# Turning q and k by transposing DMAs in place of TensorE transposes, in a windowed attention with a feed-forward layer

## The chip, the cores and the metric

The kernel runs on one core of a Trainium2 chip. A core has a matrix engine (TensorE, PE in the profile, its weight loads PEld), a vector engine (VectorE, DVE), an activation engine (ScalarE, ACT), GpSimd (POOL) and SyncE (SP), each with a queue of its own that is worked off in order, and 16 DMA engines that all queues share. SBUF is the memory that all engines work from, PSUM the one that TensorE writes into. The metric is the device time of one execution in microseconds, the median of several runs.

## The reference, cut to what matters

Eight batches of attention with eight heads, 576 positions and 64 channels per head. The first four heads see the last 32 positions; the other four see every fourth of the last 128. Then a feed-forward layer from 512 to 2048 channels and back, with SiLU in between.

```python
scores = scale * np.matmul(q, k.transpose(0, 1, 3, 2))
rel = pos[:, None] - pos[None, :]
mask_plain = (rel >= 0) & (rel < window)                      # window = 32
mask_dil = (rel >= 0) & (rel < window * dilation) & (rel % dilation == 0)   # dilation = 4
...
attn = attn / (np.sum(attn, axis=-1, keepdims=True) + 1e-09)
return np.matmul(attn, v).astype(np.float32)
...
x = np.ascontiguousarray(attn_out.transpose(0, 2, 1, 3)).reshape(B * S, H * D)
h = x @ w_in
g = h * (1.0 / (1.0 + np.exp(-h)))
return (g @ w_out).astype(np.float32)
```

Inputs and the output are float32; the kernel computes its matrix products in float16 with sums in float32.

## The kernel before, in words

**Layouts.** A score needs q and k with the 64 channels on the partitions. For the plain heads (called `z = 0`) `qT` and `kT` hold two heads one above the other on 128 partitions, and the 576 positions along the free axis. For the dilated heads (`z = 1`) the positions are split into four classes by their remainder modulo 4; `qC` and `kC` hold two classes one above the other on 128 partitions, and the 144 positions of a class along the free axis, so that a dilated head becomes four plain ones. `kT` and `kC` have 32 columns of zeros in front. Each of the four exists twice, and batch `b` uses the one of number `b % 2`. The scores of 32 queries against 64 keys are one small matmul (L324 and L336), 72 for the plain and 80 for the dilated heads of a batch.

**Getting there, before.** `load_qk` (L95) brings q and k of a batch into SBUF with eight DMAs from POOL's queue, which convert to float16. A row of the tile `n` holds 9 (plain) or 12 (dilated) consecutive positions of a head, 2304 or 3072 bytes of the source in one piece. There are two such tiles for q and two for k, so a load waits until the batch before the previous one has been read. `transpose` (L258) turns 64 (or 48) rows at a time on TensorE, into PSUM: 36 transposes for q and 36 for k of the plain heads, 24 and 24 for the dilated ones, all at L274. Four copies for each of `z = 0` and `z = 1`, half on VectorE and half on ScalarE (L278, L287), move the results to `qT`, `kT`, `qC` and `kC` and put the positions in order.

**After the scores.** VectorE scales, masks and takes maxima (L448 to L464), ScalarE takes exponentials, one instruction per 64 columns and one that reads the sum (L496), VectorE divides (L509 to L512). `turn` (L516) transposes the probabilities on TensorE, `values` (L531) multiplies by v, and the result, `xT`, is the input of the feed-forward layer. v comes in with its own DMAs (`load_v`, L123), and parts of it are shifted to other partitions by DMAs from SBUF to SBUF (`shift_v`, L162).

**Order.** The program is written out by hand. For each batch `b` there is a loop of 16 steps of the first feed-forward product (`layer1`, L639, steps 0 to 15) and then of four or five output tiles with four steps each (`layer2`, L694, from step 16). `plan_of(b)` (L737) hangs the attention of the following batches onto these steps: `at(s, fn, ...)` means that `fn` is issued just before step `s`. In the iteration of batch `b` (from 2 on) the second batch after it gets its transposes at steps 14 and 30 and its plain scores at step 17, while the next batch gets its dilated scores at step 10 or 11 and its probabilities, turns and values in between. Iterations 0 and 1 are irregular, since the pipeline fills there. As every engine works its queue in order, a step that has to wait holds what stands behind it on that engine.

**Queues.** All loads are issued from POOL, in program order; also the shifts of v for batches 2 to 7. SP issues the shifts of v for batches 0 and 1 and one DMA per output tile (`store`, L688), which waits for VectorE's copy of that tile (L691); there are five output tiles.

**Batch 0 and batch 1.** Batch 0 has its own way in (`load_qk0`, `transpose0`), and batch 1 uses `load_qk` and `transpose`. The change leaves both as they are.

Of the kernel before, what the change touches and what calls it, by code (L numbers as in the profile page):

```python
# [8 lines left out]
F16 = mybir.dt.float16  # L9
# [6 lines left out]
P = 128  # L16
W = 32
DIL = 4
# [4 lines left out]
HF = P // 2  # L23
UR = DIL
URS = (9, 12)


@with_exitstack
def kernel(
# [9 lines left out]
    nc = tc.nc  # L39
    B, H, S, D = q.shape  # L40
# [3 lines left out]
    HH = H // 2  # L44
# [4 lines left out]
    CL = S // DIL  # L49
    UPS = [S // u for u in URS]  # L50
    HS = S // 2
# [9 lines left out]
    nat = ctx.enter_context(tc.tile_pool(name="nat", bufs=2))  # L61
# [33 lines left out]
    def load_qk(b):  # L95

        for which in (0, 1):
            t = nat.tile([P, H * 8, D], F16, tag=f"n{which}", name=f"n{which}_{b}")
            u0, u1 = 2 * URS[0], 2 * (URS[0] + URS[1])
            qk[b, 0, which] = t[:, 0:u0].rearrange("p (h u) d -> p h u d", h=2)  # L100
            qk[b, 1, which] = t[:, u0:u1].rearrange("p (h u) d -> p h u d", h=2)
        for z in (1, 0) if b == 1 else (0, 1):
            for which, src in ((1, k), (0, q)):
                for i in (0, 1):
                    h = 2 * (2 * z + i)
                    nc.gpsimd.dma_start(  # L106
                        out=qk[b, z, which][i * HF : i * HF + UPS[z]].rearrange("p h u d -> p h (u d)"),
                        in_=src[b, h : h + 2].rearrange("h (p u) d -> p h (u d)", u=URS[z]),
                    )

    def load_qk0(part):

        t0, n = ((0, PA), (SA, PB))[part]
        qk0[part] = [None, None]
        for which, src in ((1, k), (0, q)):
            t = nat.tile([P, H * 8, D], F16, tag=f"n{which}", name=f"n{which}_0{part}")
            t = qk0[part][which] = t[:, 0 : H * UR].rearrange("p (h u) d -> p h u d", h=H)
            nc.gpsimd.dma_start(
                out=t[0:n],
                in_=src[0, :, t0 : t0 + n * UR].rearrange("h (p u) d -> p h (u d)", u=UR),  # L120
            )
# [53 lines left out]
    qk = {}  # L175
# [16 lines left out]
    def clear_v(b, engine):  # L192
# [13 lines left out]
        out=band[0:W], in_=band[0:W], compare_op=ALU.is_ge, fill=NEG,  # L206
# [3 lines left out]
        out=band[0:W], in_=band[0:W], compare_op=ALU.is_ge, fill=NEG,  # L210
# [35 lines left out]
    def att(b):  # L246
        if b not in state:
            state[b] = {
                "qT": qTs[b % 2],
                "kT": kTs[b % 2],  # L250
                "qC": qCs[b % 2],
                "kC": kCs[b % 2],
                "vw": vws[b % 2],
                "xT": xtp.tile([P, HP, S], F16, tag="xT", name=f"xT_{b}"),
            }
        return state[b]

    def transpose(b, z, which, copies):  # L258
# [3 lines left out]
        a = att(b)  # L262
        src, n, ur = qk[b, z, which], UPS[z], URS[z]
        ts = [ps.tile([P, ur, n], F16, tag="ps", name=f"t{which}_{b}_{z}_{i}") for i in (0, 1)]
# [457 lines left out]
    def transposes(at, b, z, step):  # L722
        for which in (1, 0):
            at(step, transpose, b, z, which, both)

    def later(at, b, z, steps, copies=(nc.vector.tensor_copy, nc.vector.tensor_copy)):

        for hi in (0, 1):
            at(steps[hi], normal, b, z, hi)
        for hi in (0, 1):  # L730
            at(steps[2], turn, b, z, hi)
        for hi in (0, 1):
            at(steps[2], turned, b, z, hi, copies[hi])
        at(steps[3], values, b, z)
        at(steps[3], finish, b, z, copies)

    def plan_of(b):  # L737
        ev = {}

        def at(s, fn, *args):  # L740
            ev.setdefault(s, []).append((fn, args))

        def all_exps(b, z):
            for hi in (0, 1):
                at(16, exps, b, z, hi)

        if b == 0:

            at(-16, normal, 0, 1, 1)
            at(-15, shift_class, 0, dve, 1, 2)  # L750
            at(-14, normal, 0, 0, 1)
            at(-13, clear_v, 1, nc.vector)
            at(-13, load_v, 1)
            for c in (2, 3):
                at(-13, load_w_out, c)
            at(-13, load_qk, 2)
            at(-8, turn, 0, 1, 1)
            at(-8, turned, 0, 1, 1, act)
            at(-6, values0, 1, 1)
            at(-6, last_values, 0, 1, (1,))  # L760
            at(-6, finish0, 1, 1)
            at(-6, last_finish, 0, 1, 1)
            at(-4, turn, 0, 0, 1)
            at(-4, turned, 0, 0, 1)
            at(-2, values0, 0, 1)
            at(-2, last_values, 0, 0, (1,))
            at(-2, finish0, 0, 1, both)
            at(-2, last_finish, 0, 0, 1)
            transposes(at, 1, 1, 2)
            at(8, scores, 1, 1)  # L770
            for hi in (0, 1):
                at(8, shift, 1, 1, hi)
            for which in (1, 0):
                at(17, transpose, 1, 0, which, (dve, dve))
            at(20, scores, 1, 0)
            at(14, shift_v, 1, nc.sync.dma_start)
            at(15, load_qk, 3)
            at(15, load_v, 2)
            at(15, shift_v, 2, nc.gpsimd.dma_start)
            all_exps(1, 1)  # L780
            for hi in (0, 1):
                at(20, exps, 1, 0, hi)
            for n, z, hi in ((20, 1, 0), (20, 1, 1), (26, 0, 0), (28, 0, 1)):
                at(n, normal, 1, z, hi)
            for n, z, copies in ((27, 1, (dve, dve)), (30, 0, both)):
                for hi in (0, 1):
                    at(n, turn, 1, z, hi)
                for hi in (0, 1):
                    at(n, turned, 1, z, hi, both[hi])
                at(n + 1 + z, values, 1, z)  # L790
                at(n + 1 + z, finish, 1, z, copies)
        elif b == 1:
            transposes(at, 2, 0, 2)
            transposes(at, 2, 1, 10)
            transposes(at, 3, 0, 15)
            at(7, scores, 2, 0)
            at(17, load_qk, 4)
            at(17, load_v, 3)
            at(17, shift_v, 3, nc.gpsimd.dma_start)
            at(13, scores, 2, 1)  # L800
            all_exps(2, 0)
            all_exps(2, 1)
            at(21, scores, 3, 0)
            at(21, exps, 3, 0, 0)
            at(21, exps, 3, 0, 1)
            later(at, 2, 0, (22, 24, 27, 28))
            later(at, 2, 1, (29, 31, 33, 34))
        else:
            if b + 2 < B:
                at(16, load_v, b + 2)  # L810
                at(16, shift_v, b + 2, nc.gpsimd.dma_start)
            if b + 1 < B:
                if b == 2:
                    for n in (0, 1):
                        at(1 + 2 * n, transpose, 3, 1, 1 - n, both)
                later(at, b + 1, 0, (0, 0, 4, 6))
                if b + 3 < B:
                    at(16, load_qk, b + 3)
            if b + 2 < B:
                transposes(at, b + 2, 0, 14)  # L820
                at(17, scores, b + 2, 0)
                at(18, exps, b + 2, 0, 0)
                at(18, exps, b + 2, 0, 1)
            if b + 1 < B:
                at(10 if b == 2 else 11, scores, b + 1, 1)
                all_exps(b + 1, 1)
                later(at, b + 1, 1, (22, 24, 28, 29) if b == 6 else (22, 24, 27, 28))
            if b + 2 < B:
                transposes(at, b + 2, 1, 30)

        def plan(s):
            for fn, args in ev.pop(s, ()):
                fn(*args)

        return plan
# [58 lines left out]
    for b in range(B):  # L894
        plan = plan_of(b)
        if b == 0:
            for x in range(NFF):
                plan(2 * x - NFF)
                plan(2 * x + 1 - NFF)
                layer1_part(2 * x % NFF, 2 * x // NFF, None if x else warm)  # L900
        else:
            for f in range(NFF):
                plan(f)
                layer1(b, f)
        if b == 0:
            layer2_first(plan)
        else:
            layer2(b, plan)
        for s in range(NFF, 3 * NFF):
            plan(s)  # L910
# [30 lines left out]
```

## Time and profile before

| | |
|---|---|
| median of 3 runs | 325.28 us (325.08 to 325.43) |
| profiled execution, its own time | 324.54 us |
| profiled execution, span of the profile | 322.8 us |
| granted TensorE clock | 0.999 |
| TensorE busy | 311.8 us, 97% |
| ScalarE busy | 214.7 us, 67% |
| VectorE busy | 180.1 us, 56% |
| POOL busy | 83.2 us, 26% |
| transposes at L274 | 840, for batches 1 to 7 |
| DMA packets | 45668, 32.63 MB |

In the profile a line such as `L274 PE MATMUL` names the line of the kernel, the engine and the operation. The slices cut the span into 40 equal parts, a digit gives the busy share in tenths. The chain lists, in order of time, the work that the end waited for: start, duration, engine, tile and line, and how many instructions were merged. A line of the waits gives the total time, the number of waits and the longest one. A line of the table by stretches gives, after the stretch and its length, the busy time and the number of instructions of PE, PEld, DVE, ACT and POOL, then the clock, the DMA share and GB/s.

### The profile page before, as it was taken

To read this page: it belongs to the slowest core of one execution; us is meant where nothing else is said; L and a number is where in the kernel's file an instruction comes from. 1 tells how busy PE (TensorE), PEld (TensorE's weight loads), DVE (VectorE), ACT (ScalarE), POOL (GpSimd) and SP (SyncE) were. 2 spreads that over 40 slices of the span, in tenths; PEclk is the share of its full clock that TensorE was granted. 3 is DMA by queue.
4 is the path that set the end of the run, shared out by engine and by line. 5 is a ranking of instruction groups with operands and counts; after the bars stand their busy time and mean duration, and the time that the engine had idled before them with its cause. 6 is when DMAs were issued, how large, how long until landed. Compare 5 with 4: busy or idle time off the path is not lost.

```text
span 322.8 us, 11769 instructions
## 1 busy us (share of the span) xinstructions
PE 311.8 (97%) x5151; PEld 202.0 (63%) x5151; DVE 180.1 (56%) x379; ACT 214.7 (67%) x700; POOL 83.2 (26%) x140
## 2 busy tenths in 40 slices
PE   5899999999999999999999999999999999999995
PEld 2667754677446775577645776567745776467544
DVE  5896679736597556663665446662576423620011
ACT  1776657657999569965896458975799357736300
POOL 8545537418404430335005700050000000000000
PEclk9999999999999999999999999999999999999999
DMA  8999999938924990298119840191011100110021
GB/s 108 187 212 198 184 230 204 227 99 124 184 86 83 129 146 36 73 163 133 26 68 140 170 80 2 67 174 37 5 52 49 65 4 0 68 67 0 2 97 67
DMA packets 45668, 32.63 MB, mean 101 GB/s; under 512 B 21264, under 2 KB 40336, under 8 KB 45616
## 3 DMA queue, kind: packets, MB, share of 16 engines
q0 software_dynamic: 39520, 21.73, 49.1%
q1 hardware_dynamic: 5952, 10.08, 8.5%
q8 instruction: 40, 0.66, 0.8%
q14 instruction: 12, 0.10, 0.1%
q10 hardware_dynamic: 144, 0.07, 0.1%
HBM read 37.75 MB, written 9.44 MB: 146 GB/s over the span
## 4 chain that ended last, share of the span: by engine, by line
PE 87%; DVE 6%; ACT 3%; issue 1%; POOL 1%; DMA 1%; POOLq 0%
PE h L644 35%; PE o L707 33%; PE h L664 4%; PE t L274 3%; PE x L554 3%; PE pt L521 2%; PE o L681 2%; PE s L336 2%; PE s L324 1%; DVE pn L512 1%; DVE ms L448 1%; ACT pe L496 1%; DVE nm L464 1%; PE x L580 1%; DVE ob L691 1%
## 5 line engine op out<-in xcount | busy, mean ns | idle before, releaser
L707 PE MATMUL o<-w_out,gT 128*128 128x512 f16 (+1 forms) x528 | 115.6, 373 | 0.0
L644 PE MATMUL h<-xT,w_in 128*128 128x288 f16 x896 | 115.4, 286 | 0.0
L652 ACT ACTIVATE gT<-h 128x576 f16<-128x576 f32 x112 | 72.8, 650 | 61.9 <-PE h L644 61.2
L644 PEld LDWEIGHTS <-w_in 128*128 128x128 f16 x896 | 85.7, 98 | 23.0 <-DVE xT L631 0.3
L496 ACT ACTIVATE pe<-ms,nm 128x64 f32<-128x64 f32 x246 | 81.6, 333 | 3.3 <-DVE nm L464 3.2
L707 PEld LDWEIGHTS <-gT 128*128 128x128 f16 x528 | 50.1, 98 | 53.0
L691 DVE COPY ob<-o 128x512 f32<-128x512 f32 (+1 forms) x36 | 24.6, 682 | 52.5 <-PE o L707 52.1
L496 ACT ACTIVATION_READ_ACCUMULATOR pe<-ms,nm 128x1 f32 x246 | 46.0, 187 | 0.0
L448 DVE SCALAR_TENSOR_TENSOR ms<-s,mask 128x512 f32<-128x512 f32 x28 | 19.2, 686 | 41.4 <-PE s L336 25.0
L127 POOL DMA_DIRECT2D vw<-in_v_dram x16 | 10.1, 640 | 76.9 <-PE x L554 75.5
L512 DVE TENSOR_TENSOR pn<-pe,r 128x640 f16<-128x640 f32 (+2 forms) x32 | 25.3, 792 | 1.1
L631 DVE CAST xT<-x 128x512 f16<-128x512 f32 x27 | 17.4, 686 | 12.0 <-PE xs L618 12.0
L464 DVE TENSOR_REDUCE nm<-ms 128x10 f32<-128x640 f32 (+1 forms) x28 | 22.0, 787 | 1.0
L106 POOL DMA_DIRECT2D n<-in_k_dram x28 | 16.5, 602 | 14.6 <-PE t L274 5.2
L106 POOL DMA_DIRECT2D n<-in_q_dram x28 | 16.4, 605 | 10.0 <-DMA w_out<-in_moe_w_out_dram 5.4
L664 PE MATMUL h<-xT,w_in 128*128 128x256 f16 (+1 forms) x128 | 17.9, 295 | 0.5 <-ACT gT L671 0.5
L529 DVE COPY ptT<-pt 128x640 f16<-128x640 f16 (+1 forms) x27 | 11.7, 468 | 8.0 <-PE pt L521 8.0
L664 PEld LDWEIGHTS <-w_in 128*128 128x128 f16 x128 | 12.5, 101 | 4.7 <-issue 1.2
L681 PE MATMUL o<-w_out,gT 128*128 128x512 f16 x64 | 15.1, 380 | 0.0
L671 ACT ACTIVATE gT<-h 128x512 f16<-128x512 f32 (+1 forms) x16 | 10.3, 650 | 7.1 <-PE h L664 6.9
L521 PE MATMUL pt<-ident,pn 128*128 128x128 f16 x152 | 12.4, 224 | 1.4 <-DVE pn L512 1.2
L521 PEld LDWEIGHTS <-pn 128*128 128x128 f16 x152 | 10.1, 99 | 4.7 <-DVE pn L512 1.5
(102 smaller groups left out, 267.6 us busy)
## 6 DMA issues: line engine op xcount, KB each, us to landing
out_dram<-ob SPq DMA_DIRECT2D x35, 256.0 KB, 2.1
n<-in_k_dram POOLq DMA_DIRECT2D x28, 144.0 KB, 5.4
n<-in_q_dram POOLq DMA_DIRECT2D x28, 144.0 KB, 5.5
vw<-in_v_dram POOLq DMA_DIRECT2D x8, 288.0 KB, 6.7
vw<-in_v_dram POOLq DMA_DIRECT2D x16, 128.0 KB, 4.8
w_in<-in_moe_w_in_dram POOLq DMA_DIRECT2D x4, 512.0 KB, 11.6
w_out<-in_moe_w_out_dram POOLq DMA_DIRECT2D x4, 512.0 KB, 10.6
vw<-vw POOLq DMA_DIRECT2D x12, 128.0 KB, 2.8
```

The lines of the kernel that those rows point to most:

```text
L106: nc.gpsimd.dma_start(out=qk[b, z, which][i * HF : i * HF + UPS[z]].rearrange("p h u d -> p h (u d)"), in_=src[b, h : h + 2].rearrange("h ...
L448: nc.vector.scalar_tensor_tensor(out=ms[:, 0:8].rearrange("p (n t) c -> p n (t c)", n=2), in0=s[hi].rearrange("p n t c -> p n (t c)"), sca ...
L464: nc.vector.tensor_reduce(out=nm[:, 0:w], in_=ms[:, 0:w], axis=AX.X, op=ALU.max, negate=True)
L496: nc.scalar.activation(pe[:, t, :], slot(t), AF.Exp, scale=1.0 if b else scale, bias=nm[:, t : t + 1], accum_out=l[:, t : t + 1],)
L512: nc.vector.tensor_tensor(pn[:, 0:w], a["pe", z, hi][:, 0:w], r[:, 0:w, None].broadcast_to([P, w, KB]), ALU.mult)
L521: nc.tensor.transpose(t[:, i, :], a["pn", z, hi][:, 2 * i : 2 * i + 2].rearrange("p t c -> p (t c)"), ident)
L644: nc.tensor.matmul(h[:, half, 0:HS], w_in16[:, c, f * P : f * P + P], xT[:, c, half * HS : half * HS + HS], start=(c == 0), stop=(c == MC ...
L652: nc.scalar.activation(gT[:, f, s0 : s0 + S].rearrange("p (a c) -> p a c", a=2), h[:, :, 0:HS], AF.Silu)
L664: nc.tensor.matmul(h[:, i, 0 : c1 - c0], w_in16[:, c, (f + i) * P : (f + i + 1) * P], xT[:, c, c0:c1], start=(c == 0), stop=(c == MC - 1),)
L681: nc.tensor.matmul(o, gT[:, f, t * P : (t + 1) * P], w_out16[:, f, :], start=(f == 0), stop=(f == NFF - 1),)
L691: copy(ob, o)
L707: nc.tensor.matmul(o, gT[:, f, t * P : (t + 1) * P], w_out16[:, f, m0:m1], start=(f == 0), stop=(f == NFF - 1),)
```

## The change

For batches 2 to 7, `load_qk` and `transpose` are replaced by `load_rows` and `cross`.

`load_rows` keeps the tile `n` and the conversion to float16, but lays it out by rows of tokens. For the plain heads a DMA per head puts position `64 m + p` on partition `p`; the columns are ordered by pair of heads, `m`, head within the pair, channel. Each piece of the source is the 64 channels of one position, 256 bytes. For the dilated heads one DMA puts the positions `4 i` to `4 i + 3` of all four heads on partition `i` for `i` up to 127, and a second one does the last 16, on partitions 64 to 79; the pieces are 1024 bytes. That is six DMAs for k and six for q.

`cross` issues transposing DMAs from SP's queue, from SBUF to SBUF. For the plain heads one DMA for each pair of heads and each of k and q takes 64 rows of 1152 columns, nine groups of 128 columns, and writes the 128 partitions of `qT` or `kT`. For the dilated heads one takes 128 rows of 1024 columns and one the last 16 rows, straight into `qC` or `kC`. That is eight transposing DMAs per batch. TensorE, PSUM, VectorE and ScalarE have no part in it.

In the schedule, `cross` for batch 2 stands at steps 22 and 25 of iteration 0, behind SP's shifts of v for batch 1; for the batch `b + 2` it stands at steps 2 (plain) and 6 (dilated) of iteration `b`. Scores, exponentials and all the rest stay at their steps.

```diff
+RT = 64
...
+    def load_rows(b):
+
+        for which, src in ((1, k), (0, q)):
+            t = nat.tile([P, H * 8, D], F16, tag=f"n{which}", name=f"n{which}_{b}")
+            f = t[0:RT].rearrange("p u d -> p (u d)")[:, 0 : 2 * S // RT * P]
+            f = qk[b, 0, which] = f.rearrange("p (i m h d) -> p i m h d", i=2, h=2, d=D)
+            for h in range(HH):
+                nc.gpsimd.dma_start(
+                    out=f[:, h // 2, :, h % 2], in_=src[b, h].rearrange("(m p) d -> p m d", p=RT)
+                )
+            f = t.rearrange("p u d -> p (u d)")
+            u0, n = 2 * S // RT * P, HH * DIL * D
+            f = qk[b, 1, which] = [f[:, u0 : u0 + n], f[RT : RT + CL - P, 0:n]]
+            for e, (o, i0) in enumerate(zip(f, (0, P))):
+                nc.gpsimd.dma_start(
+                    out=o.rearrange("p (h c) -> p h c", h=HH),
+                    in_=src[b, HH:H].rearrange("h (p r) d -> p h (r d)", r=DIL)[i0 : i0 + o.shape[0]],
+                )
+
+    def cross(b, z):
+
+        a = att(b)
+        for which in (1, 0):
+            f = qk[b, z, which]
+            if z == 0:
+                for i in (0, 1):
+                    o = (a["qT"], a["kT"][:, :, W:])[which][:, i]
+                    nc.sync.dma_start_transpose(
+                        out=o.rearrange("d (m p) -> d m p", p=RT),
+                        in_=f[:, i].rearrange("p m h d -> p (m h d)"),
+                    )
+            else:
+                for i0, g in zip((0, P), f):
+                    o = (a["qC"], a["kC"][..., W:])[which][..., i0 : i0 + g.shape[0]]
+                    nc.sync.dma_start_transpose(out=o.rearrange("d h m i -> d (h m) i"), in_=g)
...
-            at(-13, load_qk, 2)
+            at(-13, load_rows, 2)
...
+            at(22, cross, 2, 0)
+            at(25, cross, 2, 1)
...
-            at(15, load_qk, 3)
+            at(15, load_rows, 3)
...
-            transposes(at, 2, 0, 2)
-            transposes(at, 2, 1, 10)
-            transposes(at, 3, 0, 15)
+            at(2, cross, 3, 0)
+            at(6, cross, 3, 1)
...
-            at(17, load_qk, 4)
+            at(17, load_rows, 4)
...
-                if b == 2:
-                    for n in (0, 1):
-                        at(1 + 2 * n, transpose, 3, 1, 1 - n, both)
...
-                    at(16, load_qk, b + 3)
+                    at(16, load_rows, b + 3)
...
-                transposes(at, b + 2, 0, 14)
+                at(2, cross, b + 2, 0)
+                at(6, cross, b + 2, 1)
...
-            if b + 2 < B:
-                transposes(at, b + 2, 1, 30)
```

## The prediction

> **What bounds the kernel now.** I read the page first, engine shares and slices; then the chain in order of time, for what a transpose costs the engine that sets the end; then the engines' own waits; last the DMA stretches, since the change moves its work there.
>
> ```profile
> PE 311.8 (97%) x5151; PEld 202.0 (63%) x5151; DVE 180.1 (56%) x379; ACT 214.7 (67%) x700; POOL 83.2 (26%) x140
> DMA  8999999938924990298119840191011100110021
> PE 87%; DVE 6%; ACT 3%; issue 1%; POOL 1%; DMA 1%; POOLq 0%
> ```
>
> TensorE works 97% of the 322.8 us span and carries 87% of the chain. The DMA engines are the second thing to watch: nine tenths or more in most slices up to about 65 us, then bursts.
>
> ```profile
> 190.98 3.05 PE h L644 x24
> 194.03 0.76 PE t L274 x72
> 194.78 2.07 PE h L644 x16
> ...
> 209.35 1.83 PE o L707 x8
> 211.18 0.71 PE t L274 x48
> 211.89 1.83 PE o L707 x8
> 213.72 3.92 PE h L644 x32
> ```
>
> This stretch of the chain shows the work that goes: 72 transposes of the plain heads (0.76 us) and 48 of the dilated heads (0.71 us) per batch, squeezed between feed-forward matmuls with no gap. It also shows a restart: 32 uninterrupted matmuls of L644 take 3.92 us (0.1225 each), so 24 should take 2.94 and took 3.05, 16 should take 1.96 and took 2.07. Each switch back costs 0.1 us (the same for L707: 8 take 1.83 against 40 in 8.74).
>
> ```profile
> SPq L692 <- DVE ob L691: 233.1, 29, 23.8
> ...
> POOL vw L127 <- PE x L554: 75.5, 4, 24.4
> ...
> POOL n L106 <- PE t L274: 5.2, 1, 5.2
> ```
>
> The SP queue and POOL mostly wait: SP for output tiles, POOL for buffers of v. Both have room; the only wait of a q or k load on the transposes is one of 5.2 us, at 73 us; it becomes a wait for batch 2's transposing DMAs, with v of batch 3 queued behind it.
>
> ```profile
> 60.00:65.00 5.00, 5.00 (x104) 3.62 (x103) 2.87 (x5) 4.58 (x8) 1.03 (x2) 1.00 1.54 236
> 65.00:70.00 5.00, 5.00 (x109) 3.88 (x108) 0.69 (x1) 3.00 (x5) 1.07 (x2) 1.00 0.51 129
> 70.00:75.00 5.00, 5.00 (x85) 3.93 (x83) 3.73 (x7) 3.67 (x6) 1.90 (x4) 1.00 0.11 10
> ```
>
> The last two columns are the DMA share (packets overlap, so it can pass 1) and GB/s. The initial backlog ends at about 66 us. From there each batch of q, k and v is a burst of some 16 us in 36.
>
> **The change, part by part.**
>
> *Transposes on TensorE removed.* In the chain the groups of batches 2 to 7 are 0.76, 0.70, 0.52 + 0.61, 0.40, 0.40, 0.76, 0.71, 0.76, 0.71, 0.76, 0.71, 0.76 and 0.70 us: 9.26 us for 720 matmuls. They are 13 interruptions, each with a restart of 0.1: 1.3 us more. As TensorE has no idle before them, all 10.6 us is on the path.
>
> *Copies out of PSUM removed.* 48 copies, on VectorE 0.75 us and ScalarE 0.64 us each, four of either per batch: 3.0 and 2.6 us per batch. Worth nothing directly: TensorE hides them. They matter as cover: ScalarE's exponentials fill the second layer (17.64 us busy of the 21 from 157 to 178), and a shorter TensorE could have met them. At the turn after batch 2 ScalarE copies from 137.08 to 138.27, loads its table until 139.56, and then waits 0.60 us for L644. TensorE gives up 0.81 there, ScalarE 1.2: the slack stays. VectorE ends batch 4's probabilities at 142.2, 0.9 us before TensorE turns them at 143.07; both move together, since they follow the same output copy. What is late next is thus the operands of the scores.
>
> *Loads by rows.* Per batch 8 loads become 12. Each plain head is read as 576 pieces of 256 B, 4608 per batch, and the dilated heads as 1152 of 1 KB, instead of 896 pieces of 2.3 or 3 KB. Nearest row: the plain part of v (L140) has 2304 such pieces, takes POOL 1.19 us and landed in 5.1 us where the DMA was quiet (209 to 213 us); L127, 256 pieces of 1 KB, takes 0.63. So on POOL 8 x 0.72 + 2 x 0.70 + 2 x 0.57 = 8.3 us in place of 4.8: hidden, POOL is busy 26%. In transfer, q and k now take about 9 us (145 to 154 us); v's plain pieces took some 4 us, so I take 8.5 + 4 = 12.6 us, 4 more per batch. Bounds: no more (as many bytes) and 2 x 5.1 + 5 = 15 us.
>
> *Transposing DMAs on SP.* Eight per batch: four of 64 x 1152, two of 128 x 1024, two of 16 x 1024. No row shows one. From below they are copies from SBUF to SBUF, as the shifts of v: 0.51 us of the queue and 2.2 us to land. From above each lands before the next begins, at the 5.5 us that such copies took under load: 44 us per batch. By pieces of 256 B there are 4608 a batch; L140's 5.1 us less the 2.2 us floor is 1.26 ns a piece, so 5.8 us of transfer per batch. I take that, with 1.2 us of the queue each (the longest shift, L160 on SP, took 1.22) and a landing of 5.5 us in the backlog, 3 us after it. They are nearest to the shifts: same memory at both ends, same queue.
>
> The Trainium skill (Advanced Engine Details and Errata, X-Bar Transpose (TRN2)) says that transposing DMAs run as fast as plain ones, 350 to 400 GB/s. An estimate from it for 1.18 MB is 3.4 us per batch, and the total would then be about 1.5 us below mine; no run yet shows it.
>
> *SP's queue.* In the steady state the transposes enter right after the last store of the batch before, 8 x 1.2 = 9.6 us, and the next store is due some 20 us into the batch; five output tiles give more room. The plain scores are due at step 17, some 17 us in. Hidden, while four transposes take under about 14 us.
>
> *The beginning is not so roomy.* Due times are those of before less the transposes already gone. Batch 2: loads landed at 54.2 (48.76 + 5.4), now 58; plain operands are there at 57 + 2 x 1.2 + 5.5 = 65, due 67.9; dilated ones at 57 + 8 x 1.2 + 5.5 = 72, due 74.5. Batch 3: loads landed at 60.5, now 4 + 4 for two batches' rows + 6 for batch 2's transposes later, 74.5; operands at 82.4, due 82.6. Batch 3's v hangs behind: POOL shifts v of batch 2 when it lands (66.5, now 80.5), then issues 12 loads of batch 4 to 90, their bytes and the rest of batch 3's transposes last to 98, v of batch 3 to 104, its shifts land at 107.5, and L554 wants them at 106 (109.97 less 3.9). So 1.5 us of stall; bounds 0 (rows at no cost) and 9 (the 14 us of delay come to 22 if loads and transposes cost their upper values). Afterwards POOL waits 12 to 24 us per batch for buffers, and the delay is absorbed.
>
> Sum on the profiled execution: 324.54 - 10.6 + 1.5 = 315.4 us. The median of the runs is 325.28, 0.74 above it: 316.2 us.
>
> **The rivals.**
>
> *Backlog.* The rows and transposes of batches 2 and 3 fill the DMA engines to 100 us or beyond, and TensorE waits 4 to 9 us at batch 3's plain scores or at its values. For: slices at 9 up to 65 us, landings of 6.5 to 13.6 us for q and k loads issued before 46 us. Against: a stall gives its length to every later due time. Worst, 324.54 - 10.6 + 9 + 0.74 = 323.7; typically 321.
>
> *Slower: the transposes pass one after another.* SP issues in order and holds the next until the last has nearly landed. Cost c each: 48 of them from 53 us on, then the 58 us from the dilated scores of the last batch (264.78) to the end: 53 + 48c + 58. It decides from c = 4.45 us, where this is 324.5; at 5.5 it is 375. Below that, c over 3.5 us makes the plain scores late, at step 17. For: in the crowded part the shifts from SP took 5.3 to 7.4 us to land. Against: that is landing time, and the trace shows shifts issued 0.6 us apart. The Trainium skill (VectorE: DVE Perf Modes, The three transpose paths) gives 1309 ns for a 128 x 128 block by DMA against 390 ns on TensorE. If blocks passed one by one, 36 per batch would make 47 us and the whole 53 + 6 x 47 + 58 = 393 us, an estimate that falls on this side; the page does not say whether blocks overlap.
>
> *All hidden.* No stall at all: 314.7 us. For: the lateness above, 1.5 us, is smaller than the error of its terms.
>
> *ScalarE becomes the bound.* It would leave about half the gain, 320 us; the 0.60 us wait and the copies that it loses speak against.
>
> **How the numbers follow.** Forecast (0 to 4 us of stall, all hidden included) 0.54, backlog 0.17, ScalarE 0.02, no change within 0.2% (0.65 us, about what a measurement of this kernel can tell) 0.03, slower through the transposes 0.24. So faster 0.73, same 0.03, slower 0.24. The likeliest alone spans 314.2 to 319. The range goes on through the backlog to a transpose price just past the deciding point: 314.2 to 327; the slow tail beyond it is about 0.19.
>
> **What would show it.** TensorE's groups of L274 shrink to batch 1's 120; its busy time falls by 9 to 11 us; no wait of TensorE on a transposing DMA beyond some 1.5 us at batch 3; a queue time on SP of about 1.2 us per transpose, landing under 6. Wrong if SP holds each transpose for over 3.5 us, if the scores of batches 4 to 7 wait for DMA, if stores queue so long that VectorE waits for output tiles, or if the DMA slices stay at 9 beyond 110 us.

## The result, and the profile after

The changed kernel takes 321.86 us (median of 20 runs, 317.59 to 326.83) against 324.78 us before (20 runs, 323.39 to 326.35). The medians thus differ by 2.9 us. The ratio used here and below leaves out every run that is over 1.5% above the fastest of its kernel; it is 0.9845, with a 95% interval of 0.9816 to 0.9875, so that 5.0 us (4.1 to 6.0) come off. Forecast were 9.1: the change is faster and inside the range, but it gives about half of that, and by the medians a third. The runs of the changed kernel scatter over 9 us, those of before over 3, and part of what follows bears on that. Its profiled execution took 322.74 us, with a span of 321.0.

From the page of the changed kernel: engines (busy time, share, instructions), granted clock and DMA by slices, the DMA queues (packets, MB, share) and the shares of the chain.

```profile
PE 304.5 (95%) x4431; PEld 195.8 (61%) x4431; DVE 163.0 (51%) x355; ACT 201.4 (63%) x676; POOL 106.8 (33%) x164
...
PEclk9999999999999999999879999999999999999999
DMA  8999999999999999799914999279501100110021
...
q0 software_dynamic: 69088, 21.74, 72.7%
q1 hardware_dynamic: 33792, 17.16, 27.1%
q8 instruction: 34, 0.56, 0.7%
...
PE 81%; DVE 6%; DMA 6%; ACT 3%; issue 2%; POOL 1%; SPq 1%; POOLq 0%
```

TensorE has the 720 matmuls less, but its busy time fell by only 7.3 us, and its share of the span from 97 to 95%: it works less and also stands more. Two slices show a lower clock. The DMA engines stay at nine tenths to 160 us, but for one slice, and come back to it from 176 to 200; before, they left that level at 65 us. "issue" has grown to 2% of the chain: time in which the engine waits for nothing that the profile shows.

The stretches that ended the backlog before now do not (same columns, changed kernel):

```profile
60.00:65.00 5.00, 5.00 (x53) 3.51 (x42) 1.69 (x4) 3.93 (x6) 2.45 (x5) 1.00 2.44 141
65.00:70.00 5.00, 5.00 (x109) 3.91 (x107) 1.19 (x2) 2.69 (x5) 2.24 (x4) 1.00 1.88 177
70.00:75.00 5.00, 5.00 (x79) 3.88 (x78) 1.81 (x4) 3.35 (x6) 0.48 (x1) 1.00 1.27 282
```

The share falls from 2.44 to 1.27 only, where it fell from 1.54 to 0.11.

TensorE's waits in the changed kernel (total us, times, longest):

```profile
PE s L361 <- issue: 3.0, 1, 3.0
PE s L373 <- issue: 1.5, 1, 1.5
...
PE s L361 <- DMA qT<-n: 0.6, 1, 0.6
```

The only wait for a transposing DMA is the 0.6 us at the plain scores of batch 3, at 83.2 us. The two long ones have no releaser. The chain of the changed kernel around the longer of them (start, duration, what), and the same pieces of a later batch:

```profile
154.35 0.86 PE o L744 x4
155.21 0.43 PE s L361 x42
155.64 2.99 issue
158.63 0.36 PE s L361 x20
158.99 0.11 PE ss L361 x8
159.09 11.49 PE o L744 x40
...
192.71 5.01 PE h L681 x40
197.72 0.86 PE o L744 x4
198.58 0.61 PE s L361 x64
199.19 0.08 PE ss L361 x6
199.27 8.74 PE o L744 x40
```

In the later batch nothing stands between L744, the 64 scores and L744 again: no transposes, as intended. In the earlier one TensorE stops in the middle of the scores, after 42 of 64, for 2.99 us, and then 40 matmuls of L744 take 11.49 us in place of 8.74. The table by stretches of the changed kernel says why (columns as for the kernel before):

```profile
155.00:156.00 1.00, 0.64 (x43) 0.36 (x42) 0.00 (x0) 0.98 (x2) 0.09 (x1) 1.00 3.21 99
156.00:157.00 1.00, 0.00 (x0) 0.00 (x0) 0.00 (x0) 0.99 (x5) 0.00 (x0) 1.00 8.88 72
157.00:158.00 1.00, 0.00 (x0) 0.00 (x0) 0.00 (x0) 1.00 (x8) 0.00 (x0) 0.91 0.38 21
158.00:159.00 1.00, 0.37 (x30) 0.30 (x30) 0.00 (x0) 1.00 (x8) 0.00 (x0) 0.50 2.41 152
```

The granted clock goes to 0.50, and the trace keeps it there for 6.83 us. In the stall the DMA share is 8.88 at 72 GB/s, and in the next microsecond 21 GB/s are moved: packets that begin there stay open for long. One packet that comes late is TensorE's own. Queue q8 of the page carries packets of 16384 bytes, 34 now and 40 before; TensorE has 8862 matmuls and weight loads now and 10302 before, one packet for each 256. Counting all of TensorE's instructions in the trace from the first (matmuls, weight loads and a few on semaphores), every long "issue" gap of the changed kernel and of its variants below falls on instruction 256 n + 193, at the end of such a block:

```
run                gap, us (length)        instruction       its packet, us   TensorE goes on
changed kernel     112.50-113.96 (1.46)  3777 = 14*256+193   111.39-112.66    1.3 us after it
changed kernel     155.64-158.63 (2.99)  5057 = 19*256+193   155.25-157.10    1.5
b2_wide_loads      204.11-207.62 (3.51)  6081 = 23*256+193   204.54-205.97    1.6
b3_again           112.00-114.17 (2.17)  3777 = 14*256+193   110.83-112.30    1.9
c3_hybrid           63.51- 64.73 (1.22)  2241 =  8*256+193    62.49- 63.47    1.3
d2_plus64           63.70- 67.18 (3.48)  2241 =  8*256+193    64.55- 65.82    1.4
gaps that wait for data: 2809, 2945, 3481 (not of the form 256 n + 193)
```

TensorE had run out of instructions. The packet for the next block leaves some time after the boundary before it: 0.9 us (median) where the DMA engines have room, and up to 160 us in the changed kernel mostly 1.8 to 6.5 us, 3.3 in the median. It then takes 0.9 to 2.3 us, and after a gap TensorE goes on some 1.4 us behind its end. A block that TensorE goes through faster than this round trip ends in a gap. Blocks with scores, turns and values in them are short: the one that ends at 112 us takes some 5 us. The kernel before has blocks as short, 4.8 us up to 63.1 and 3.5 us up to 79.6, but there the packet left 1.8 and 0.7 us after the boundary, and none of its matmuls waits for "issue". What holds a packet back before it leaves, the traces do not show; they show only that it is late where the DMA engines are crowded.

The Trainium skill (Runtime: NRT & Kernel Launch, Instruction fetch mechanics) says that instructions come in blocks of 256 over a DMA queue of the sequencer's own, while the current block runs, at a cost that is mostly hidden. The trace agrees on the size and on the queue; the cost is hidden in the kernel before, and not in the changed one. The Trainium skill (TensorE: Matmul & The Clock Gate, Why this matters for your kernels) warns of idle gaps over some 3 us, behind which the clock is halved. The gap of 2.99 us agrees; of two shorter ones below, 2.13 us in `d1_plus40` was enough as well, for half as long, and 2.17 us in `b3_again` was not.

### The profile page after: what moved, and what is told of

Same layout as the page of the kernel before. It is cut to its first block, busy times and chain, and to the rows that moved or that the text cites. A ratio compares the mean times of both kernels' runs of the same rounds, so it can differ in the third digit from the quotient of the medians.

```text
span 321.0 us, 10444 instructions
## 1 busy us (share of the span) xinstructions
PE 304.5 (95%) x4431; PEld 195.8 (61%) x4431; DVE 163.0 (51%) x355; ACT 201.4 (63%) x676; POOL 106.8 (33%) x164
## 3 DMA queue, kind: packets, MB, share of 16 engines
q1 hardware_dynamic: 33792, 17.16, 27.1%
## 4 chain that ended last, share of the span: by engine, by line
PE 81%; DVE 6%; DMA 6%; ACT 3%; issue 2%; POOL 1%; SPq 1%; POOLq 0%
PE h L681 33%; PE o L744 32%; PE h L701 4%; DMA qT<-n 3%; PE x L591 3%; PE pt L558 2%; DMA n<-in_q_dram 2%; PE o L718 2%; PE s L361 1%; DVE pn L549 1%; PE s L373 1%; DVE ms L485 1%; SPq L139 1%; ACT pe L533 1%; DVE nm L501 1%
## 5 line engine op out<-in xcount | busy, mean ns | idle before, releaser
L744 PE MATMUL o<-w_out,gT 128*128 128x512 f16 (+1 forms) x528 | 117.7, 379 | 0.0
L681 PE MATMUL h<-xT,w_in 128*128 128x288 f16 x896 | 113.8, 286 | 0.0
L744 PEld LDWEIGHTS <-gT 128*128 128x128 f16 x528 | 51.1, 99 | 55.8 <-issue 3.3
L119 POOL DMA_DIRECT2D n<-in_q_dram x24 | 17.8, 774 | 10.4 <-DMA w_out<-in_moe_w_out_dram 5.0
L119 POOL DMA_DIRECT2D n<-in_k_dram x24 | 17.8, 760 | 2.5 <-PE h L701 2.0
```

Source lines behind the costliest of these rows:

```text
L119: nc.gpsimd.dma_start(out=f[:, h // 2, :, h % 2], in_=src[b, h].rearrange("(m p) d -> p m d", p=RT))
L681: nc.tensor.matmul(h[:, half, 0:HS], w_in16[:, c, f * P : f * P + P], xT[:, c, half * HS : half * HS + HS], start=(c == 0), stop=(c == MC ...
L744: nc.tensor.matmul(o, gT[:, f, t * P : (t + 1) * P], w_out16[:, f, m0:m1], start=(f == 0), stop=(f == NFF - 1),)
```

## The experiments

The first three separate the parts of the change: `a0_same` runs it again, `b1_no_cross` takes the transposing DMAs away and keeps the loads by rows, `b2_wide_loads` keeps the transposing DMAs and takes the loads by rows away.

**a0_same.** No edit.

> The changed kernel once more. Theory F (TensorE's own instructions, fetched in 16 KB packets on DMA queue 8, come late where the DMA engines are crowded, and a stall of about 3 us also halves the clock for some 7 us): the spread of 317 to 327 us comes back, with TensorE gaps released by 'issue' at other places than in the first profile (there 1.46 us at 112.5 and 2.99 us at 155.6), each beginning within 1 us of the start of a packet on queue 8. Theory D (the operands come late, always at the same scores): the same gaps at the same places, and times within 1 us of one another.

Measured: 320.6 us (318.58 to 326.15, 6 runs), ratio 0.9848 [0.9822, 0.9875]. TensorE's waits:

```profile
PE s L373 <- issue: 3.5, 1, 3.5
...
PE x L591 <- DMA vw<-vw: 0.9, 1, 0.9
```

One gap without a releaser, 3.47 us at 112.83, again at instruction 3777; its packet started at 113.59, when TensorE already stood. Waits for data are 0.35 us at batch 3's plain scores and 0.88 us at its values. The spread and the late packet are as theory F has them, but the place is one of the first profile's, as theory D has it; only moving the block ends, further below, tells the two apart.

**b1_no_cross.** `cross` issues nothing, so the scores of batches 2 to 7 are computed from what lies in the buffers.

```diff
     def cross(b, z):
-        a = att(b)
-        for which in (1, 0):
+        att(b)
+        for which in ():
```

> Loads by rows as changed, but no transposing DMA at all: the scores of batches 2 to 7 are made from what batches 0 and 1 left in the operands, so the output is not the reference's. What TensorE is spared stays. Theory F with the transposes as the larger part of the crowding: 313.5 to 315 us (324.5 less the 10.6 us), runs within 1.5 us of each other, no gap released by 'issue' over 1 us. Rival R (the small pieces of the row loads alone are the trouble): 316 us and more, gaps by 'issue' remain and the runs spread as before.

Measured: 313.55 us (313.41 to 314.29, 4 runs), ratio 0.9661 [0.9648, 0.9674]. From its page:

```profile
PE 301.0 (97%) x4431; PEld 194.7 (62%) x4431; DVE 163.2 (52%) x355; ACT 201.4 (65%) x676; POOL 106.7 (34%) x164
...
DMA  8999999999995995299319990291011000200021
```

This is the change with no transposes at all: 11.2 us below before, and TensorE's busy time is 10.8 us lower. With the block ends where they are here, rows alone cost TensorE next to nothing. It also gives a yardstick: its matmuls are those of the changed kernel one for one, so each can be held against its twin. What the profiled executions lose against it, by the time at which a matmul falls behind:

```
                           changed kernel       a0_same
waits for data             0.59  (83 us)        0.36 (83) + 1.04 (107)
gap at a block boundary    1.69 (112) + 3.14 (156)   3.70 (112)
half clock behind it       2.81                 2.60
all, to the end            9.2                  8.4
```

Of the 9.2 us, 7.6 are late instructions and the half clock that follows them.

**b2_wide_loads.** The loads of before in pieces of 2.3 and 3 KB, and the same eight transposing DMAs per batch on the bytes that they bring (in an order that is not that of the tokens).

```diff
     def load_rows(b):
+        load_qk(b)
...
+            qk[b, 0, which] = [t[i * RT : i * RT + RT, 0:n] for i in (0, 1)]
+            qk[b, 1, which] = [t[:, 0:g], t[RT : RT + CL - P, 0:g]]
```

> Loads in pieces of 2.3 and 3 KB as in the kernel before, and the eight transposing DMAs of the changed kernel per batch, of the same shapes, from those bytes: the operands are permuted, so the output is not the reference's. Theory F: the crowding is less by the 4 us or more per batch that the rows cost, 314.5 to 317 us, spread about half. Rival X (transposing DMAs themselves, whatever the loads, hold up the instruction fetch): 318 to 322 us with gaps by 'issue' as in the changed kernel. Rival R: 314 to 315 us, no spread.

Measured: 328.7 us (325.52 to 334.27, 7 runs), ratio 1.0074 [1.0049, 1.0099]: slower than before, and above all that was expected. TensorE's waits, and the transposes to `kC`, in the profiled execution, which is the slowest of the seven:

```profile
PE s L352 <- DMA qT<-n: 8.2, 3, 5.3
PE s L352 <- issue: 3.5, 1, 3.5
```

```profile
L136 SPq DMA_TRANSPOSE kC<-n x12: 1222/2116/7707, 58.7 to 235.0; - x12
```

I had taken the rows to be the dearer part. With large pieces SP holds a transpose for up to 7.7 us, and TensorE waits 8.2 us for operands. That small packets of the transposes queue behind large ones of the loads would explain it, but no run separates this.

**b3_copies.** Each transposing DMA is replaced by a plain copy from SBUF to SBUF, in pieces of 256 bytes, from the same queue at the same place; q and k are not turned. The copies carry nine tenths of the bytes, since they leave out one of the nine column groups of the plain heads and a part of the last 16 rows.

```diff
-                    nc.sync.dma_start_transpose(
-                        out=o.rearrange("d (m p) -> d m p", p=RT), ...
+                    nc.sync.dma_start(
+                        out=o.rearrange("p (b c) -> p b c", b=8)[:, :, 0:P], ...
```

> The changed kernel with each of the 48 transposing DMAs replaced by a plain copy from SBUF to SBUF, at the same place of SP's queue, from the same rows to the same operand tiles, in pieces of 256 bytes (8 of the 9 column groups of the plain heads, and of the last 16 rows a part); the operands are thus not turned and the output is not the reference's. Theory T (turning in flight is what makes the DMA engines stand still and TensorE's instruction packets late): 313.5 to 315.5 us, close to the 313.6 us without any such DMA, no gap of TensorE released by 'issue', no stretch in which no DMA packet ends. Rival C (any further traffic of 256-byte packets does it): 318 to 322 us, with gaps by 'issue', as the changed kernel's 320.6.

Measured: 317.41 us (314.66 to 319.05, 4 runs), ratio 0.9757 [0.9716, 0.9798]. It was run again:

> The kernel of b3_copies once more (plain copies in pieces of 256 B in place of the transposing DMAs; what TensorE then computes with is not q and k turned). If plain traffic of this size has a price of its own, 316 to 319 us again, with gaps without a releaser of under 2 us and no stretches in which all packets stand still. If the slower executions of b3_copies were chance, 313.5 to 315, beside b1_no_cross.

Measured: 316.37 us (314.62 to 317.22, 4 runs), ratio 0.9724 [0.9695, 0.9754]. The first of these lines is of `b3_again`'s waits of TensorE, the second of `b3_copies`' copies to `kT` (min, median, max on SP, in ns), the third of the transposes to `kT` in the changed kernel:

```profile
PE s L375 <- issue: 2.2, 1, 2.2
```

```profile
L139 SPq DMA_DIRECT2D kT<-n x12: 596/608/686, 49.4 to 207.9; - x12
```

```profile
L139 SPq DMA_TRANSPOSE kT<-n x12: 1200/1311/4122, 49.3 to 216.5; - x12
```

The 2.2 us are again at instruction 3777; the profile of `b3_copies`, its fastest execution, has 0.4 us there. Both medians lie between what theory T and what rival C had expected. So plain traffic of about this size already makes instructions late and costs 2.8 to 3.9 us against `b1_no_cross`, and turning the bytes another 3.2 to 4.2 against `a0_same`. Two differences can be seen: SP needs twice as long for a plain head's transpose, and there are stretches of over 0.15 us in which at least four packets are open and none ends. The trace has 1 of them before (0.26 us in all), none and 1 with copies, 3 without either (0.48), and 20 (5.3 us) and 16 (4.9) in the two profiles of the changed kernel. That these stretches are what makes the transposes dearer is not shown.

**c1_early.** If the packets are late in the stretch where loads and transposes meet, the transposes of batches 4 to 7 could go earlier.

```diff
+            at(20, cross, 4, 0)
+            at(22, cross, 4, 1)
...
+                    at(20, cross, b + 3, 0)
+                    at(22, cross, b + 3, 1)
...
-                at(2, cross, b + 2, 0)
-                at(6, cross, b + 2, 1)
```

> The changed kernel with the transposing DMAs of batches 4 to 7 issued one iteration earlier, at steps 20 and 22, right behind the row loads of the same batch, so that they no longer run beside the row loads of the next one. Theory F: fewer packets in flight at once, so fewer and shorter 'issue' gaps: 315 to 318 us, most runs at a clock of 1.0. If the crowding is a matter of the sum and not of the overlap: 318 to 322, as the changed kernel. If SP's stores, which now stand behind transposes that wait for their loads, hold VectorE: over 322.

Measured: 322.25 us (319.85 to 325.01, 6 runs), ratio 0.9909 [0.9875, 0.9943]: worse than the change as it was. No gap at a block boundary is left after 60 us, but there is a new wait of TensorE:

```profile
PE x L591 <- DMA vw<-vw: 5.9, 2, 4.8
```

Batch 3's v stands behind the transposes that were pulled forward. The values fall 6.15 us behind `b1_no_cross`, and half clock adds 2.2.

**c2_v_first.** The early place for batches 5 to 7 only, and v of batch 3 ahead of the rows of batch 4: `load_rows` stays at step 17 but now stands behind `load_v` and `shift_v` of batch 3.

```diff
-            at(17, load_rows, 4)
...
+            at(17, load_rows, 4)
...
+                    at(20, cross, b + 3, 0)
+                    at(22, cross, b + 3, 1)
...
+                if b == 2:
+                    at(2, cross, 4, 0)
+                    at(6, cross, 4, 1)
+                at(18 if b == 2 else 17, scores, b + 2, 0)
```

> The edit of c1_early for batches 5 to 7 only. For batch 4 the transposing DMAs stay at steps 2 and 6 of iteration 2 (plain scores at 18 in place of 17), and in iteration 1 the loads and shifts of v of batch 3 go ahead of the loads of the rows of batch 4. If what was left of the loss in c1_early was the late v of batch 3 (4.75 + 1.17 us of waits on vw, then 6.8 us at half clock, which costs some 2.75 us), no wait on vw is left and the time is 314.5 to 317 us. If the transposes of batch 4 land too late for step 18, TensorE waits 1 to 3 us on a transposing DMA at the first scores of batch 4 and the time is 317 to 319. If it is any stretch in which transposing DMAs meet loads that holds back TensorE's instruction packets, wherever the two are put, gaps without a releaser of 1 us or more come back near 100 to 115 us and the time is 318 to 321.

Measured: 319.01 us (316.0 to 324.63, 6 runs), ratio 0.9823 [0.9777, 0.9869]. The wait for v is gone; the profiled execution, 316.0 us and the fastest of the six, is 2.5 us behind `b1_no_cross`, 1.01 of it for data at batch 3's scores and 1.23 at instruction 3777. The median lies above the 314.5 to 317 that were expected for a cure, where the third case of the expectation has it, and its interval overlaps that of the change.

**c3_hybrid.** `c1_early`, with batch 2 turned on TensorE as before.

```diff
-            at(-13, load_rows, 2)
+            at(-13, load_qk, 2)
...
-            at(22, cross, 2, 0)
-            at(25, cross, 2, 1)
...
+            transposes(at, 2, 0, 2)
+            transposes(at, 2, 1, 10)
```

> The kernel with the early transposing DMAs for batches 4 to 7 (steps 20 and 22 of the iteration before), with batch 2 back to the loads in wide pieces and the TensorE transposes of the kernel before, so that the crowded beginning has one batch of rows and transposing DMAs less. It gives back batch 2's 1.46 us of transposes and two restarts. If the remaining loss of the early variant is batch 3's v that lands late behind the backlog (4.75 and 1.17 us of waits and then half clock): no such wait, 315 to 317 us, most runs at full clock. If the loss only moves (another operand late, or gaps by 'issue'): 319 to 322 us.

Measured: 319.5 us (317.57 to 320.76, 6 runs), ratio 0.9825 [0.9793, 0.9857]. TensorE's waits:

```profile
PE s L361 <- issue: 1.2, 1, 1.2
PE t L311 <- issue: 1.2, 1, 1.2
...
PE x L591 <- issue: 0.5, 1, 0.5
```

The gaps now stand before a transpose, a score and a value, at 63.5, 70.8 and 102.3 us: with 72 + 48 transposes back, the blocks end elsewhere. All three are at 256 n + 193. That led to the next runs, which move the block ends alone.

**d1_plus40, d2_plus64, d3_c2_plus40.** 40 or 64 small matmuls more at the very beginning (41 or 65 for one of the long ones), so that each later instruction stands 80 or 128 places further on and the block ends fall on earlier work. (The expectations count by the old numbers: 256 n + 113 and + 65 there are 256 n + 193 in the new count.)

```diff
+    def shift_fetch(tile, n):
+
+        for _ in range(n):
+            nc.tensor.matmul(
+                tile[0:32, 0, 0:16], ident[:, 0:32], ident[:, 0:16], start=True, stop=True
+            )
...
-    keep_busy(big.tile([P, 2, 512], F32, tag="big", name="busy"), 4)
+    busy = big.tile([P, 2, 512], F32, tag="big", name="busy")
+    keep_busy(busy, 3)
+    shift_fetch(busy, 41)
```

> The changed kernel with 40 TensorE matmuls more at the beginning (the fourth warming matmul of 0.47 us replaced by 41 small ones in the time in which TensorE waits anyway), so that every boundary between blocks of 256 TensorE instructions falls 80 instructions earlier in the program. In the runs so far every gap without a releaser lies at instruction 256 n + 193, at the end of a block that TensorE went through in 4.9 to 6.7 us. Theory B (a block is asked for at the boundary before, and TensorE stands when its round trip over the crowded DMA engines takes longer than the block): the block that ends at 112 us now takes 6.3 us in place of 4.9, the shortest one is 5.75 us near 62 us; the gap at 112 is gone or under 0.7 us, any gap lies at 256 n + 113, and the time falls by 1 to 2 us, to 317.5 to 320. Rival G (something else holds TensorE at the scores of these batches, and the packet is late with it): gaps of 1.5 to 3.5 us stay in front of the same scores at 112 us, 320 to 322 us.

Measured: 320.91 us (319.36 to 321.61, 6 runs), ratio 0.9877 [0.9852, 0.9901].

```profile
PE h L681 <- issue: 2.1, 1, 2.1
...
PE s L361 <- issue: 1.1, 1, 1.1
PE x L617 <- issue: 0.9, 1, 0.9
```

> As d1_plus40, with 64 matmuls more: boundaries 128 instructions earlier. Theory B: the shortest block is then 3.9 us and ends near 60 us, where the round trip of an instruction packet takes some 6 us: a new gap of 2 to 3 us there, at 256 n + 65, none at 112 (the block there takes 6.7 us); the time is 319.5 to 322. Rival G: no gap near 60, the gap at 112 as in the changed kernel.

Measured: 324.68 us (322.07 to 327.01, 12 runs), ratio 0.9984 [0.9959, 1.001].

```profile
PE x L591 <- issue: 3.5, 1, 3.5
...
PE x L617 <- issue: 1.5, 1, 1.5
```

> c2_v_first with the 40 matmuls more. Theory B: the gap of 1.0 us at 112 goes, a small one near 62 may come; what stays are the 1.0 us on the first scores of batch 3 and the packets that stand still: 316 to 318.5 us. Rival G: as c2_v_first, 319.

Measured: 320.95 us (319.21 to 321.61, 6 runs), ratio 0.9876 [0.9848, 0.9904].

```profile
PE h L681 <- issue: 3.3, 2, 1.8
```

The places came as theory B had them, with one more in `d3_c2_plus40`, where the two gaps lie at 64.1 and 80.0 us. The gap at 112 us is gone in all three. In `d2_plus64` the block that ends near 62 us ends in one of 3.48 us, in front of values; in `d1_plus40` there is one of 2.13 us at 65.6, in the middle of feed-forward matmuls that wait for nothing else. Nothing holds TensorE at the scores in particular: rival G falls. The sizes did not come: `d1_plus40` was to take 317.5 to 320 us, `d2_plus64` 319.5 to 322 and `d3_c2_plus40` 316 to 318.5, and all three are slower. Held against `a0_same` matmul by matmul, `d1_plus40` is 7.5 us behind at 83 us, 1.9 of it from before 45 us, 1.5 from 48 to 56 us and 4.0 from the gap at 65.6 and the half clock behind it; then it gets 6.3 back at 112 us, where `a0_same` has its gap and its half clock, and 1.1 where that one waits for v. Of three places for the block ends, each met some short block in a crowded stretch. `d2_plus64`, whose shortest block, up to 63.7 us, takes some 4 us, uses up the whole gain of the change; it also has a gap of 1.0 us at 194 us, in a later burst of loads and transposes.

**d4_no_cross_plus64.** The last question is whether transposing DMAs are needed for a gap at all. So the 65 small matmuls go into `b1_no_cross`.

```diff
-    keep_busy(big.tile([P, 2, 512], F32, tag="big", name="busy"), 4)
...
+    keep_busy(busy, 3)
+    shift_fetch(busy, 65)
```

> b1_no_cross (rows loaded, no transposing DMAs, so that the scores of batches 2 to 7 are computed from what lies in the buffers) with the 64 matmuls more of d2_plus64. If plain loads alone are enough to make instruction packets late for a short block (theory B without any part of the transposes): in b1_no_cross the packet near 62 us left 3.9 us after the boundary before it, took 1.0, and TensorE went on 1.4 after it, 6.3 us against a block that now takes 3.9; so a gap of some 2.4 us near 62 us at instruction 2241, others of 0.5 to 1 us before 50 us, none later, where the packets leave 0.9 us after the boundary; 315.5 to 317.5 us. If it takes transposing DMAs: no gap at 2241, 313.3 to 314.3 us as b1_no_cross.

Measured: 317.86 us (317.21 to 318.12, 4 runs), ratio 0.9784 [0.9757, 0.981]. The chain of `d4_no_cross_plus64`, early:

```profile
18.43 0.41 PE x L617 x15
18.84 1.51 issue
20.35 0.38 PE x L617 x10
```

Against `b1_no_cross` it is 4.3 us slower by the medians, and 0.4 above what was expected. In the two profiles the small matmuls take 0.95 us, the boundary at 18.8 us costs 1.7, and those at 34.8, 41.1 and 63.1 us 0.4 to 0.5 each; from 67 us on the distance is constant, 3.73 us. So plain loads alone are enough early in the program: up to 49 us the packets leave 3.3 to 4.2 us after the boundary. At 63 us, where I expected a gap of 2.4 us, it was 0.2: the packet left after 2.0 us, not 3.9. What transposing DMAs and the copies in their place add is that late packets go on to 160 us, and in single cases to 204 us.

## Why the prediction was right, and where it was wrong

**Transposes removed, 10.6 us: right.** In the changed kernel only batch 1's transposes are left. From the rows of tile `t`:

```profile
L311 PE MATMUL t<-ident,n x120: 179/192/214, 31.9 to 42.7; 64*64 64x64 f16 x72, 48*128 48x48 f16 x48
```

`b1_no_cross`, the change with nothing in the transposes' place, is 11.2 us faster than before, with TensorE 10.8 us less busy. In the changed kernel it is 7.3 us less busy; 2.8 of the difference are the half clock.

**Copies worth nothing, ScalarE not the bound: right.** No wait of TensorE on ScalarE over 0.8 us is in the profile after, and `b1_no_cross` has ScalarE at the same 201.4 us without a loss.

**The stall at the beginning, 1.5 us: right in place, and in size to about 1 us.** 0.59 us at batch 3's plain scores in one profile; 0.36 there and 1.04 at batch 3's values in the other. The sum put all of it at the values and had the scores in time by 0.2 us. TensorE's waits at the scores ended at 83.8 and 83.3 us, and the one at the values at 107.6; the sum had the operands at 82.4 and v at 107.5.

**SP's queue, 1.2 us per transpose: right for the plain heads, and 1.3 to 1.6 us for the dilated ones; landing 3 to 5.5 us: too low.** Rows of the changed kernel, the first of tile `qT`:

```profile
L139 SPq DMA_TRANSPOSE qT<-n x12: 1200/1254/2276, 53.0 to 220.4; - x12
```

```profile
L146 SPq DMA_TRANSPOSE kC<-n x12: 1158/1636/2987, 56.0 to 223.3; - x12
...
DMA to landing us min/median/max: 4.8/8.5/9.6
```

Landing took 7.0 us in the median for `qT` and 8.5 for `kC`. It did not matter, since step 17 leaves some 17 us. Both queues had room as forecast. The first line is of SP's waits, the second of POOL's:

```profile
SPq L729 <- DVE ob L728: 125.5, 23, 20.9
```

```profile
POOL vw L164 <- PE x L591: 40.7, 3, 17.6
```

**The rival "one after another": refuted.** It needed 4.45 us for each transpose; the medians are 1.2 to 1.6 us of SP's queue and the longest 4.1, and only `b2_wide_loads` shows more. The Trainium skill's 1309 ns for a 128 x 128 block (VectorE: DVE Perf Modes, The three transpose paths) is thus no price of blocks in a row: 36 such blocks a batch leave SP in some 10 to 13 us. The Trainium skill's sentence that transposing DMAs are as fast as plain ones (Advanced Engine Details and Errata, X-Bar Transpose (TRN2)) roughly holds here for the landing: to `kT` 6.1 us, against 5.1 and 5.8 for the copies of `b3_copies` and `b3_again`, which carry eight ninths of the bytes. It does not tell the price for the rest: SP was held 1.3 us in place of 0.6, and the kernel with the copies was 3.2 to 4.2 us faster.

**Transfer of rows and transposes: too low by the queues' shares, near by the arrivals.** I added 4 us per batch for rows and 5.8 for transposes. By the shares of the queues, q0 rose from 49.1% of 322.8 us to 63.9% of 311.7 in `b1_no_cross`, 41 us or 6.8 per batch, past the upper bound of 6; q1 rose from 8.5% to 27.1%, 60 us or 10 per batch. Packets that are open and wait count here too, so these are no prices of the transfer alone: with 6.8 + 6.8 + 10 in place of 4 + 4 + 6 us the sum would have had batch 3's operands at 92 us, where they came at 83 to 84. The slices stayed at 9 to 160 us, one of the signs named for a wrong forecast.

**What failed: the last line of the sum.** It read "324.54 - 10.6 + 1.5", with the argument that "afterwards POOL waits 12 to 24 us per batch for buffers, and the delay is absorbed". The delay of data was absorbed. But TensorE's own instructions come over the same DMA engines, and the sum had no term for them: 4.8 us of gaps at block boundaries and 2.8 us of half clock in one profile, 3.7 and 2.6 in the other. The sum for a profiled execution, 315.4, and these 7.6 and 6.3 us give 323.0 and 321.7; the two took 322.74 and 321.89. The backlog rival had this size, 321 to 323.7, with a wrong mechanism: it had TensorE wait for scores' operands or values. That 321.86 us lies inside the stated range is therefore luck: the span of the forecast itself, 314.2 to 319, missed it. The question that I asked of the DMA backlog was when data land, and never who else uses the engines. The row was there: the page of before lists the same instruction queue with 40 packets.

**The scatter.** How late a packet is, and whether the clock then halves, differs from execution to execution. In the same kernel the gaps were 1.46 and 2.99 us in one profile and 3.47 us in the other, and `b1_no_cross`, which has none, scatters over 0.9 us. That this makes the whole scatter is argued and not shown: the mean clock does not order the 20 runs, as the fastest, 317.59 us, and the slowest, 326.83, both ran at 0.984.

## What to carry to other kernels

Before moving work from an engine to the DMA engines, count all their users, the engines' own instruction packets among them: here the gaps of 0.3 us and more all came behind blocks of 256 instructions that TensorE ran through in 4 to 7 us, too short to cover a late packet. A gap "issue" at one instruction number modulo 256, with a packet of the instruction queue ending 1 to 2 us before TensorE goes on, is the sign to look for. Run the change with the new transfers left out: the distance between that and the real one is what the transfers cost, in late data and in crowding, and holding the two kernels' matmuls against each other one by one shows where.

## What the hardware showed that I had not expected

- TensorE stops at every 256th instruction if the next block's packet is late: the profiles of the changed kernel and its variants have 26 "issue" waits of 0.3 to 3.5 us, all of them at such a boundary. The packet leaves 0.9 us after the boundary before when the DMA engines have room and up to 6.5 us after it when they are crowded, in `b2_wide_loads` 7.2.
- After the start of the program, a gap of TensorE of 2.1 us or more was followed in all cases but one by a granted clock of 0.5 for 3.4 or 6.8 us, which costs up to 2.8 us more: 40 matmuls in 11.49 us in place of 8.74. The exception is the 2.17 us of `b3_again`.
- 64 small matmuls at the beginning of a program moved its time by 4.3 us (`d4_no_cross_plus64` against `b1_no_cross`; 3.7 between the two profiles, 0.95 of it their own and the rest through the places of the block ends).
- Transposing DMAs from SBUF to SBUF come with stretches in which packets stand still, 3.4 to 5.8 us per execution in all profiles that have them; plain copies of nine tenths of the bytes show under 0.2 us.
